# Splitting the k columns 512 and 130 instead of 322 and 320, in a TensorE-bound attention and state-space kernel

## The chip, the cores and the metric

One Trainium2 chip, one core of it. The metric is the device time of one execution in microseconds (us); a profiled execution gives the trace from which the rows in this text come. TensorE is PE in the rows, its weight loads PEld, VectorE is DVE, ScalarE is ACT, GpSimd is POOL and the queue that issues the DMAs is SP.

## What is computed

The input x has 2048 rows of 640 columns. Two branches are mixed by a gate:

```
g = sigmoid((x * gate_w).sum(-1))
a = y + x * Dskip                     # y: x convolved with K, K from A, B, C, dt
q, k, v = split(x @ wqkv)             # 32 heads of 20
pq, pk = phi(q), phi(k)               # phi(t) = (t + 1 if t > 0 else exp(t)) + 1e-6
kv = einsum(pk, v); z = pk.sum(over rows)
o = (pq @ kv) / (pq @ z + 1e-6)
out = g * a + (1 - g) * (o @ wo)
```

The kernel uses that pk.T @ v equals (pk.T @ x) @ wv: it collects G = pk.T @ x, or its transpose, over all rows, and multiplies by wv and wo afterwards.

## The kernel before

Every large product is made of three matmuls: an operand is split into a rounded high part (fp32r, a copy on ACT or DVE, `hi`) and a low part (what is left, a subtraction on DVE or POOL, `lo`), and the product is high by high, low by high and high by low (`mm3`, L105).

The kernel runs in three stages, in an order written out by hand.

**First tiles (L444 to L514).** The 2048 rows are 16 tiles of 128. The first four tiles' k is computed block by block while the blocks arrive from memory: a block is 128 of the 640 inner columns, so there are five blocks. For each block SP loads a piece of xT and of the k weights (L476 to L488), ACT, DVE and POOL split them (L489 to L496), and `k_first` (L447) issues the matmuls. Here xT is the stationary operand (128 by 128, loaded into TensorE before each matmul) and the k weights are the moving one. The 640 columns of k and the two columns of gate_w that ride along, 642 in all, are two halves: `wkA` of 322 columns (the gate's two at its end) and `wkB` of 320. Each half of each of the four tiles has a PSUM bank of its own, eight in all. `wkA` is done for all five blocks, tiles inside a block; `wkB` for blocks 0 and 1 in the same way, and for blocks 2 to 4 tile by tile at the end (L505).

**The k loop (L536 to L605).** For tile T it computes k (`k_mm`, one half, then the other, 15 matmuls each; for T of 4 and more), applies phi (`k_act`: Exp and Relu on ACT, a combination on DVE), splits pk (`k_split` on DVE), and adds tile T-1 to G: `g_main` (L220) has x as stationary operand and the first 512 columns of pk as moving one, five blocks of 3 matmuls; `g_rest` (L232) makes the other 128 columns of pk the stationary operand and has x's 640 columns as moving one, in two pieces of 320, 3 matmuls each. The order on TensorE in one turn is k half 0 of T, block 0 of `g_main`, blocks 1 and 2, k half 1 of T, `g_rest`, blocks 3 and 4. In the last turn the weights of q are split into the places that k's weights held (L561, L596): three blocks of 128 columns in `wqA`, two in `wqB`. The result of `g_rest` is then copied out (L613) and transposed on TensorE (`rem_out`, L626) into the last columns of `GT`.

**The q stage (L729 on).** A written plan interleaves q blocks, the products with wv and wo, the normalisation and the final product; its matmuls have 512 moving columns (the last output block 256 twice).

Of the kernel before, what the change touches and what calls it, by code (L numbers as in the profile page):

```python
# [30 lines left out]
F32 = mybir.dt.float32  # L31
F32R = mybir.dt.float32r
I32 = mybir.dt.int32
AF = mybir.ActivationFunctionType
# [5 lines left out]
P = 128  # L40
L = 2048
D = 640
NB = D // P
# [1 line left out]
NG = L // 512  # L45
H = 32
DH = 20
CA, CB = 320, 320
GRP = [(i * 120, min(120, D - i * 120)) for i in range(6)]
HC = 60  # L50
EPS = 1e-6
# [1 line left out]
NY = 6  # L53
NWARM = 7
N0 = 4
CONV_P = {1: (0, 1), 2: (2, 3), 3: (4,)}
CONV_K = {5: (0, 1), 6: (2, 3), 7: (4,), 8: (5, 6), 9: (7, 8), 10: (9,), 11: (10, 11), 12: (12, 13), 13: (14,)}
NK = sum(map(len, CONV_K.values()))
WQ = 3, 4, 0, 1, 2
QI = DH // NB  # L60
WKO = 40


PLAN = """
# [14 lines left out]
def body(tc, i, outT):  # L79
# [19 lines left out]
    def hi(dst, src):  # L99
        act.activation(dst, src, AF.Copy)  # L100

    def lo(dst, src, h, eng=None):
        (eng or dve).tensor_tensor(dst, src, f32(h), op=OP.subtract)  # L103
# [6 lines left out]
    def col(tag, n=NB, dt=F32):  # L110
        return pc.tile([P, n], dt, tag=tag, name=tag)

    def w_tiles(n, tag, name):
        return tuple(pc.tile([P, NB, n], F32R, tag=tag + x, name=name + x) for x in "hl")
# [22 lines left out]
    s_all = col("s_all", NT)  # L137
    ident = col("ident", P)
    bdm = col("bdm", HC)
    kvz = [col(f"kvT{k}", P) for k in range(3)]  # L140
    for v in kvz:
        pool.memset(v, 0.0)
    dtc, k0, dsk, lam, ok = [col(n) for n in ("dtc", "k0", "dsk", "lam", "ok")]
# [40 lines left out]
    kp, ke, ks = {}, {}, {}  # L184

    def k_mm(t, hf, tag="k"):
        whl, nw = (wkA, CA + 2) if hf == 0 else (wkB, CB)
        gi, o = divmod(t, 4)
        s = slice(o * P, o * P + P)
        kp[t, hf] = bank(tag)  # L190
        for b in range(NB):
            mm3(kp[t, hf][:, :nw], xTh[gi][:, b, s], xTl[gi][:, b, s],
                whl[0][:, b, :nw], whl[1][:, b, :nw], b == 0, b == NB - 1)

    def k_act(t, hf):

        p, c0, n = kp.pop((t, hf)), hf * CA, (CA, CB)[hf]
        if hf == 0:
            ke[t] = pk.tile([P, D], F32, tag="e", bufs=3, name="e")
        e = ke[t][:, c0 : c0 + n]  # L200
        r = pk.tile([P, CA], F32, tag="r", bufs=2, name="r")
        act.activation(e, p[:, :n], AF.Exp)  # L202
        act.activation(r[:, :n], p[:, :n], AF.Relu)  # L203
        if hf == 0:
            act.activation(s_all[:, t : t + 1], p[:, CA : CA + 1], AF.Copy)
        dve.scalar_tensor_tensor(e, e, 1.0, r[:, :n], op0=OP.min, op1=OP.add)  # L206

    def k_split(t):
# [23 lines left out]
    def g_rest(t):  # L232

        (xh, xl), (h, l) = xs[t], ks[t]
        if t == 0:
            for n in (0, 1):
                gps["r", n] = bank(f"r{n}")
        for n in (0, 1):
            s = slice(n * 320, n * 320 + 320)
            o = gps["r", n][:, :320]  # L240
            pe.matmul(o, h[:, 512:], xh[:, s], start=t == 0, stop=False)
            pe.matmul(o, h[:, 512:], xl[:, s], start=False, stop=False)  # L242
            pe.matmul(o, l[:, 512:], xh[:, s], start=False, stop=t == NT - 1)  # L243
# [200 lines left out]
    FIRST = {(0, 0): "g0", (0, 1): "g1", (1, 0): "g2", (1, 1): "r0",  # L444
             (2, 0): "r1", (2, 1): "g3", (3, 0): "g4", (3, 1): "k"}

    def k_first(b, hf, tiles, passes):  # L447

        w, n = ((wkA, CA + 2), (wkB, CB))[hf]
        for ps in passes:  # L450
            for t in tiles:
                if (t, hf) not in kp:
                    kp[t, hf] = bank(FIRST[t, hf])
                sl = slice(t * P, t * P + P)
                pe.matmul(kp[t, hf][:, :n], (xTl if ps == 1 else xTh)[0][:, b, sl], w[ps // 2][:, b, :n],  # L455
                          start=b + ps == 0, stop=b == NB - 1 and ps == 2)

    wkA = tuple(v[:, :, WKO : WKO + CA + 2] for v in w_tiles(3 * P, "wA", "wkA"))
    wkB = w_tiles(CB, "wB", "wkB")
    raw = {}  # L460

    x0 = {}
    xTh[0] = px.tile([P, NB, 512], F32R, tag="xh0", name="xTh0")
    xTl[0] = px.tile([P, NB, 512], F32R, tag="xl0", name="xTl0")
    cuts = {b: (0, 2, N0) if b == 0 else (0, N0) for b in range(NB)}
    pieces = {b: [slice(t0 * P, t1 * P) for t0, t1 in zip(cuts[b], cuts[b][1:])] for b in cuts}

    def wkB_load(b):
        sp.dma_start(raw[b][:, CA + 2 :], i["wkB"][b])

    def wkB_split(b):
        w = raw.pop(b)[:, CA + 2 :]
        hi(wkB[0][:, b, :], w)
        lo(wkB[1][:, b, :], w, wkB[0][:, b, :])

    for b in range(NB):  # L476
        x0[b] = pw.tile([P, 512], F32, tag="y", bufs=NY, name="x0")
        raw[b] = w_raw(b)
        for n, s in enumerate(pieces[b]):
            sp.dma_start(x0[b][:, s], i["xT"][b * P : b * P + P, s])  # L480
            if n == 0:
                sp.dma_start(raw[b][:, : CA + 2], i["wkA"][b])
        if b < 2:
            wkB_load(b)
    for b in range(2, NB):
# [1 line left out]
    x_load(0)  # L487
    x_load(1)  # L488
    for b in range(NB):  # L489
        w = raw[b][:, : CA + 2]  # L490
        for s in pieces[b]:
            hi(xTh[0][:, b, s], x0[b][:, s])
        dve.tensor_copy(wkA[0][:, b, : CA + 2], w)
        for s in pieces[b]:
            lo(xTl[0][:, b, s], x0[b][:, s], xTh[0][:, b, s])
        lo(wkA[1][:, b, : CA + 2], w, wkA[0][:, b, : CA + 2], pool)  # L496
        for t0, t1 in zip(cuts[b], cuts[b][1:]):
            k_first(b, 0, range(t0, t1), (0, 1))
        k_first(b, 0, range(N0), (2,))
        if b < 2:  # L500
            wkB_split(b)
            k_first(b, 1, range(N0), (0, 1, 2))
    for b in range(2, NB):
        wkB_split(b)
    for t in range(N0):  # L505
        for b in range(2, NB):
            k_first(b, 1, (t,), (0, 1, 2))
    for t in range(N0):
# [16 lines left out]
    def wq_lo(*a):  # L525
        src, h, l = wq_views(*a)
        lo(l, src, h)

    def wq_split(w, c, b0, b1, both=True):

        src, h, l = wq_views(w, c, b0, b1)
        hi(h, src)
        if both:
            lo(l, src, h)

    for T in range(1, NT):  # L536

        if T + 1 < NT:
            x_load(T + 1)
        if T + 3 < NT:  # L540
            xT_load(T + 3)
        for b in CONV_P.get(T, ()):
            conv_load(b)
        if T in (7, 8, 9, 10, 11):
            sp.dma_start(Wv[:, T - 7, :], i["wv"][(T - 7) * P : (T - 6) * P, :])
        if T == 14:
            for b in WQ:
                raw[b] = w_raw(b)
                sp.dma_start(raw[b][:, :CA], i["wqA"][b])
                sp.dma_start(raw[b][:, CA:D], i["wqB"][b])  # L550

        if T >= N0:
            k_mm(T, 0)
            k_act(T, 0)
        g_main(T - 1, (0,))
        if T == max(CONV_P) + 2:
            for j in range(3):
                u_load(j)
        if T >= 2:
            x_split(T)  # L560
        if T == NT - 1:  # L561
            wqA = w_tiles(3 * P, "wA", "wqA")
            for c in WQ:
                wq_split(wqA, c, 0, 3, c in WQ[:2])
        rest = (1, 2)
        if T == max(CONV_P) + 2:
            g_main(T - 1, rest[:1])
            conv_sum()
            rest = rest[1:]
        if N0 <= T + 2 < NT:  # L570
            xT_split(T + 2)
        g_main(T - 1, rest)
        if T >= N0:
            k_mm(T, 1)
            k_act(T, 1)
        if T > 1:
            k_split(T)
        g_rest(T - 1)
        g_main(T - 1, (3, 4))
        xs.pop(T - 1), ks.pop(T - 1)  # L580

        if T == 2:
            act.activation(dtc, dtc, AF.Exp)
            dve.tensor_reduce(zh, ident.rearrange("p (h i) -> p h i", i=QI), axis=AX.X, op=OP.add)
            dve.tensor_copy(bm.rearrange("p (h i) -> p h i", i=QI), zh[:, :, None].to_broadcast([P, H, QI]))
        for b in CONV_P.get(T - 1, ()):
            conv_block(b)()
        if T == max(CONV_P) + 1:
            conv_finish()
        if T == max(CONV_P) + 2:  # L590
            conv_scale()
        for j in CONV_K.get(T, ()):
            conv_out(j)
            if j + 3 < NK:
                u_load(j + 3)
        if T == NT - 1:  # L596
            wqB = w_tiles(CB, "wB", "wqB")
            for c in WQ[2:]:
                wq_lo(wqA, c, 0, 3)
            for c in WQ:  # L600
                wq_split(wqB, c, 3, NB)
                raw.pop(c)
            gates()
            for gi in range(NB):
                wo_load(gi)  # L605
# [4 lines left out]
    g_rest(NT - 1)  # L610
    g_main(NT - 1, (3, 4))
    rem = col("rem", D)
    hi(rem[:, :320], gps.pop(("r", 0))[:, :320])  # L613
    hi(rem[:, 320:], gps.pop(("r", 1))[:, :320])
    g_out(3, act)
    g_out(4, dve)
    kst.close()
# [1 line left out]

    pq = mk(top, "pq")  # L620
    pqp = mk(top, "pqp", PSUM)

    def mbank(name):
        return pqp.tile([P, 512], F32, tag="m", bufs=2, name=name)
# [11 lines left out]
    def q_block(gi, b):  # L636

        qp = pqp.tile([P, 512], F32, tag="q", bufs=3, name="qp")
        w, o = (wqA, b * P) if b < 3 else (wqB, (b - 3) * P)
        for c in range(NB):  # L640
            mm3(qp, w[0][:, c, o : o + P], w[1][:, c, o : o + P], xTh[gi][:, c, :], xTl[gi][:, c, :],
                c == 0, c == NB - 1)
# [301 lines left out]
```

## Time and profile before

| what | value |
|---|---|
| median of 3 runs | 300.05 us (299.36 to 300.11) |
| the profiled execution | 299.84 us, of which the span in the trace is 298.1 us |
| first matmul on data | 4.38 us |
| end of the first tiles' k on TensorE | 23.44 us |
| end of the last `g_main` | 146.15 us |
| busy | PE 98%, PEld 86%, DVE 77%, ACT 40%, POOL 16% |

A matmul's duration in a row is longer than what it costs in a stream, since matmuls overlap: what counts is the step from the start of one to the start of the next. The rows of the timeline merge neighbours of one kind ("x10"), so a step is a difference of starts divided by the number of matmuls between.

### The profile page before, as it was taken

How to read it: one execution, taken by the hardware profiler on the slowest of the kernel's cores; microseconds unless marked ns; L12 is line 12 of the kernel's file. 1: busy time of each engine (PE TensorE's matmuls, PEld its weight loads, DVE VectorE, ACT ScalarE, POOL GpSimd, SP SyncE). 2: the span in 40 equal slices, each digit the busy share in tenths (PEclk: the TensorE clock that was granted, in tenths of full speed). 3: DMA queues.
4: the chain of work that ended last, by engine and by line, in shares of the span. 5: the costliest groups of instructions: out<-in, count | busy, mean ns of one | idle time of the engine just before them, and what ended most of it. 6: DMA issues, size and time to landing. Idle time of an engine off the chain costs nothing.

```text
span 298.1 us, 4538 instructions
## 1 busy us (share of the span) xinstructions
PE 293.0 (98%) x1627; PEld 255.2 (86%) x1627; DVE 228.9 (77%) x355; ACT 119.0 (40%) x250; POOL 46.7 (16%) x52
## 2 busy tenths in 40 slices
PE   8999999999999999999999999999999999999994
PEld 7998899999999999999887777888888888888884
DVE  1959977799899899964843769978684778687992
ACT  3556143544545353327524464552323233313200
POOL 3605431000000000000000000003323203242531
PEclk9999999999999999999999999999999999999999
DMA  6917376065757857362264553692425122425323
GB/s 176 322 42 233 94 231 217 1 221 154 242 200 237 243 185 204 119 201 98 58 196 142 166 190 102 217 349 87 126 51 182 31 70 70 141 73 176 124 91 111
DMA packets 28409, 46.00 MB, mean 154 GB/s; under 512 B 3771, under 2 KB 10827, under 8 KB 28383
## 3 DMA queue, kind: packets, MB, share of 16 engines
q1 hardware_dynamic: 28383, 45.66, 48.6%
q8 instruction: 15, 0.25, 0.3%
q14 instruction: 11, 0.09, 0.1%
HBM read 32.92 MB, written 12.72 MB: 153 GB/s over the span
## 4 chain that ended last, share of the span: by engine, by line
PE 92%; DVE 3%; DMA 2%; issue 1%; ACT 1%; SPq 0%; DVEq 0%
PE qp L106 8%; PE fp L108 8%; PE fp L107 8%; PE fp L106 8%; PE qp L108 8%; PE qp L107 8%; PE k L107 6%; PE k L106 6%; PE k L108 6%; PE g L230 5%; PE g L228 5%; PE g L227 5%; PE g L455 3%; DMA wraw<-in_wkB 2%; PE r L242 1%; PE r L243 1%
## 5 line engine op out<-in xcount | busy, mean ns | idle before, releaser
L440 POOL TENSOR_TENSOR yb<-yb,gb 128x512 f32<-128x512 f32 x20 | 28.4, 1423 | 217.5 <-DVE acc L657 157.7
L108 PE MATMUL fp<-pTl,Mh 128*128 128x512 f32 (+1 forms) x105 | 39.8, 379 | 0.0
L107 PE MATMUL fp<-pTh,Ml 128*128 128x512 f32 (+1 forms) x105 | 39.8, 379 | 0.0
L106 PE MATMUL fp<-pTh,Mh 128*128 128x512 f32 (+1 forms) x105 | 39.8, 379 | 0.0
L651 DVE SCALAR_TENSOR_TENSOR qe<-qe,qr 128x512 f32<-128x512 f32 x20 | 15.4, 770 | 21.5 <-ACT qr L648 21.5
L228 PE MATMUL g<-ph,xl 128*128 128x512 f32 x80 | 31.5, 394 | 0.0
L227 PE MATMUL g<-ph,xh 128*128 128x512 f32 x80 | 31.4, 392 | 0.0
L202 ACT ACTIVATE e<-k 128x320 f32<-128x320 f32 x25 | 10.9, 437 | 47.1 <-PE k L108 47.1
L100 ACT ACTIVATE pTh<-qe 128x512 fp32r<-128x512 f32 x20 | 12.6, 633 | 41.7 <-DVE qe L687 41.7
L230 PE MATMUL g<-pl,xh 128*128 128x512 f32 x80 | 26.1, 391 | 0.1
L206 DVE SCALAR_TENSOR_TENSOR e<-e,r 128x320 f32<-128x320 f32 x32 | 15.9, 502 | 12.2 <-ACT r L203 12.0
L106 PE MATMUL qp<-xTh,wqAh 128*128 128x512 f32 x60 | 23.8, 396 | 0.0
L107 PE MATMUL qp<-xTh,wqAl 128*128 128x512 f32 x60 | 23.4, 390 | 0.0
L108 PE MATMUL qp<-xTl,wqAh 128*128 128x512 f32 x60 | 23.4, 389 | 0.0
L107 PEld LDWEIGHTS fp<-pTh,Ml 128*128 128x128 f32 x105 | 19.8, 188 | 3.8
L106 PEld LDWEIGHTS fp<-pTh,Mh 128*128 128x128 f32 x105 | 19.7, 188 | 3.8
L647 ACT ACTIVATE qe<-qp 128x512 f32<-128x512 f32 x20 | 11.9, 595 | 27.7 <-PE qp L108 22.7
L108 PEld LDWEIGHTS fp<-pTl,Mh 128*128 128x128 f32 x105 | 19.7, 188 | 3.7
L103 DVE TENSOR_TENSOR pTl<-qe,pTh 128x512 fp32r<-128x512 f32 x20 | 16.1, 819 | 6.8 <-ACT pTh L100 6.3
L420 DVE TENSOR_TENSOR_SCAN y<-y,cY,zero 128x512 f32<-128x512 f32 x16 | 20.5, 1278 | 0.8 <-ACT y L419 0.8
L107 PE MATMUL k<-wkAh,xTl 128*128 128x322 f32 x60 | 18.6, 310 | 0.0
L106 PE MATMUL k<-wkAh,xTh 128*128 128x322 f32 x60 | 18.6, 309 | 0.0
(168 smaller groups left out, 714.6 us busy)
## 6 DMA issues: line engine op xcount, KB each, us to landing
xraw<-in_x SPq DMA_DIRECT2D x16, 320.0 KB, 5.2
u<-in_xT SPq DMA_DIRECT2D x20, 256.0 KB, 5.4
out_T<-o SPq DMA_DIRECT2D x19, 256.0 KB, 2.5
y_d<-y SPq DMA_DIRECT2D x16, 256.0 KB, 2.3
yb<-y_d SPq DMA_DIRECT2D x16, 256.0 KB, 3.2
xTraw<-in_xTt SPq DMA_DIRECT2D x12, 320.0 KB, 4.4
Wv<-in_wv SPq DMA_DIRECT2D x5, 320.0 KB, 6.9
Mh<-M_dh SPq DMA_DIRECT2D x5, 320.0 KB, 4.7
```

What stands on the lines that cost most here:

```text
L100: act.activation(dst, src, AF.Copy)
L103: (eng or dve).tensor_tensor(dst, src, f32(h), op=OP.subtract)
L106: pe.matmul(out, ah, bh, start=start, stop=False)
L107: pe.matmul(out, al, bh, start=False, stop=False)
L108: pe.matmul(out, ah, bl, start=False, stop=stop)
L206: dve.scalar_tensor_tensor(e, e, 1.0, r[:, :n], op0=OP.min, op1=OP.add)
L227: pe.matmul(gps[b], xh[:, s], h[:, :512], start=t == 0, stop=False)
L228: pe.matmul(gps[b], xl[:, s], h[:, :512], start=False, stop=False)
L230: pe.matmul(gps[b], xh[:, b * P : b * P + P], l[:, :512], start=False, stop=t == NT - 1)
L420: dve.tensor_tensor_scan(y, y, zero.to_broadcast([P, 512]), cY[:, c], op0=OP.add, op1=OP.add)
L440: pool.tensor_tensor(ys[j], ys[j], gbs[j // NB], op=OP.mult)
L651: dve.scalar_tensor_tensor(e, e, 1.0, r, op0=OP.min, op1=OP.add)
```

## The change

The two halves of k become `wkA` of 512 columns and `wkB` of 130: the gate's two columns lead the second half, followed by k's last 128. `g_rest` has pieces of 512 and 128 columns instead of twice 320. The q weights lie as four blocks of 128 in `wqA` and one in `wqB`, and a few of their splits move from before `k_mm`'s second half to after it. In the first tiles, block 0 of the first half is loaded, split and multiplied in two column pieces of 256, tiles 0 and 1 of the first piece ahead; blocks 3 and 4 of the first half are no longer done for all four tiles, but tile by tile, just ahead of that tile's second half. One of three small zeroed tiles is made in the q stage.

```diff
-CA, CB = 320, 320
+CA, CB = 512, 128
+NB1 = 3
-WKO = 40
+QA = CA // P
+CK = CA, CB + 2
+WB = 192
...
     def k_mm(t, hf, tag="k"):
-        whl, nw = (wkA, CA + 2) if hf == 0 else (wkB, CB)
+        whl, nw = (wkA, wkB)[hf], CK[hf]
...
-        p, c0, n = kp.pop((t, hf)), hf * CA, (CA, CB)[hf]
+        kb = kp.pop((t, hf))
+        c0, n = hf * CA, (CA, CB)[hf]
+        p = kb[:, CK[hf] - n :]
...
-        if hf == 0:
-            act.activation(s_all[:, t : t + 1], p[:, CA : CA + 1], AF.Copy)
+        if hf == 1:
+            act.activation(s_all[:, t : t + 1], kb[:, :1], AF.Copy)
...
-        for n in (0, 1):
-            s = slice(n * 320, n * 320 + 320)
-            o = gps["r", n][:, :320]
+        for n, s in enumerate((slice(0, 512), slice(512, D))):
+            o = gps["r", n][:, : s.stop - s.start]
             pe.matmul(o, h[:, 512:], xh[:, s], start=t == 0, stop=False)
             pe.matmul(o, h[:, 512:], xl[:, s], start=False, stop=False)
             pe.matmul(o, l[:, 512:], xh[:, s], start=False, stop=t == NT - 1)
...
-    cuts = {b: (0, 2, N0) if b == 0 else (0, N0) for b in range(NB)}
-    pieces = {b: [slice(t0 * P, t1 * P) for t0, t1 in zip(cuts[b], cuts[b][1:])] for b in cuts}
+    cuts = {b: (0, 256, 512) if b == 0 else (0, 512) for b in range(NB)}
+    pieces = {b: [slice(c0, c1) for c0, c1 in zip(cuts[b], cuts[b][1:])] for b in cuts}
...
-        for n, s in enumerate(pieces[b]):
+        for s in pieces[b]:
             sp.dma_start(x0[b][:, s], i["xT"][b * P : b * P + P, s])
-            if n == 0:
-                sp.dma_start(raw[b][:, : CA + 2], i["wkA"][b])
+            to = slice(s.start, s.stop + 2 * (s.stop == CA))
+            sp.dma_start(raw[b][:, to], i["wkA"][b][:, to])
...
-        for t0, t1 in zip(cuts[b], cuts[b][1:]):
-            k_first(b, 0, range(t0, t1), (0, 1))
-        k_first(b, 0, range(N0), (2,))
+        for c in pieces[b] if b < NB1 else ():
+            for s in pieces[b] if c.start == 0 else (slice(0, 512),):
+                k_first(b, 0, range(s.start // P, s.stop // P), (0, 1), c)
+            k_first(b, 0, range(N0), (2,), c)
         if b < 2:
             wkB_split(b)
             k_first(b, 1, range(N0), (0, 1, 2))
...
     for t in range(N0):
+        for b in range(NB1, NB):
+            k_first(b, 0, (t,), (0, 1, 2))
         for b in range(2, NB):
             k_first(b, 1, (t,), (0, 1, 2))
...
-            wqA = w_tiles(3 * P, "wA", "wqA")
-            for c in WQ:
-                wq_split(wqA, c, 0, 3, c in WQ[:2])
+            wqA = w_tiles(CA, "wA", "wqA")
+            for c in WQ[:3]:
+                wq_split(wqA, c, 0, QA, c in WQ[:1])
...
-            for c in WQ[2:]:
-                wq_lo(wqA, c, 0, 3)
+            for c in WQ[1:]:
+                (wq_lo if c in WQ[:3] else wq_split)(wqA, c, 0, QA)
             for c in WQ:
-                wq_split(wqB, c, 3, NB)
+                wq_split(wqB, c, QA, NB)
```

The order on TensorE at the end of the first tiles, before: `wkA` of block 4 ends for the last tiles (banks r_175 and g_177), then tile 0's second half (bank g_187).

```order
L455 MATMUL r_175<-wkAl,xTh_131 128x322
L455 MATMUL g_177<-wkAl,xTh_131 128x322
L455 MATMUL g_187<-wkBh,xTh_131 128x320
L455 MATMUL g_187<-wkBh,xTl_132 128x320
L455 MATMUL g_187<-wkBl,xTh_131 128x320
L455 MATMUL g_187<-wkBh,xTh_131 128x320
```

The same place now: block 2 ends for the last tile (bank g_178), then tile 0 (banks g_170 and g_200) has its blocks 3 and 4 of the first half and its second half.

```order
L459 MATMUL g_178<-wkAl,xTh_129 128x512
L459 MATMUL g_170<-wkAh,xTh_129 128x512
L459 MATMUL g_170<-wkAh,xTl_130 128x512
L459 MATMUL g_170<-wkAl,xTh_129 128x512
L459 MATMUL g_170<-wkAh,xTh_129 128x512
L459 MATMUL g_170<-wkAh,xTl_130 128x512
L459 MATMUL g_170<-wkAl,xTh_129 128x512
L459 MATMUL g_200<-wkBh,xTh_129 128x130
L459 MATMUL g_200<-wkBh,xTl_130 128x130
L459 MATMUL g_200<-wkBl,xTh_129 128x130
```

Tile 0's first half is complete six wide matmuls into its own turn, and its second half nine narrow ones later; the other tiles' first halves wait for their own turns.

In the k loop the order of work on TensorE is the same and the widths change. Before, at the end of k's second half and in `g_rest` (banks r_418 and r_419):

```order
L108 MATMUL k<-wkBl,xTh_461 128x320
L241 MATMUL r_418<-xh,ph 128x320
L242 MATMUL r_418<-xl,ph 128x320
L243 MATMUL r_418<-xh,pl 128x320
L241 MATMUL r_419<-xh,ph 128x320
L242 MATMUL r_419<-xl,ph 128x320
L243 MATMUL r_419<-xh,pl 128x320
L227 MATMUL g_426<-ph,xh 128x512
```

The same place now, in the same turn:

```order
L111 MATMUL k<-wkBl,xTh_474 128x130
L245 MATMUL r_431<-xh,ph 128x512
L246 MATMUL r_431<-xl,ph 128x512
L247 MATMUL r_431<-xh,pl 128x512
L245 MATMUL r_432<-xh,ph 128x128
L246 MATMUL r_432<-xl,ph 128x128
L247 MATMUL r_432<-xh,pl 128x128
L232 MATMUL g_439<-ph,xh 128x512
```

No matmul came or went: of every two, one grew to 512 columns and one shrank to 130 or 128.

SP's first loads, before:

```order
L480 DMA x_133<-in_xT 128x256
L482 DMA wraw<-in_wkA 128x322
L480 DMA x_133<-in_xT 128x256
L469 DMA wraw<-in_wkB 128x320
L480 DMA x_139<-in_xT 128x512
```

SP's first loads now:

```order
L486 DMA x_131<-in_xT 128x256
L488 DMA wraw<-in_wkA 128x256
L486 DMA x_131<-in_xT 128x256
L488 DMA wraw<-in_wkA 128x258
L474 DMA wraw<-in_wkB 128x128
L486 DMA x_138<-in_xT 128x512
```

One load more stands ahead of block 1; the bytes ahead of it are the same.

More of the change, by code (lines that the diff above doesn't have):

```diff
@@ L139, in body @@
     bdm = col("bdm", HC)
-    kvz = [col(f"kvT{k}", P) for k in range(3)]
+    kvz = [col(f"kvT{k}", P) for k in range(2)]
     for v in kvz:
@@ L445, in body, with k_first @@
              (2, 0): "r1", (2, 1): "g3", (3, 0): "g4", (3, 1): "k"}
-    def k_first(b, hf, tiles, passes):
-        w, n = ((wkA, CA + 2), (wkB, CB))[hf]
+    def k_first(b, hf, tiles, passes, cols=None):
+        w, cs = (wkA, wkB)[hf], cols or slice(0, CK[hf])
         for ps in passes:
@@ L454, in k_first @@
                 sl = slice(t * P, t * P + P)
[L455 to L459, printed above, removed]
+                pe.matmul(kp[t, hf][:, cs], (xTl if ps == 1 else xTh)[0][:, b, sl], w[ps // 2][:, b, cs],
+                          start=b + ps + cs.start == 0, stop=b == NB - 1 and ps == 2)
+    wkA = w_tiles(CA, "wA", "wkA")
+    wkB = w_tiles(WB, "wB", "wkB")
     raw = {}
@@ L471, in wkB_split @@
     def wkB_split(b):
-        w = raw.pop(b)[:, CA + 2 :]
-        hi(wkB[0][:, b, :], w)
-        lo(wkB[1][:, b, :], w, wkB[0][:, b, :])
+        w = raw.pop(b)[:, CA:]
+        h, l = [v[:, b, : CK[1]] for v in wkB]
+        hi(h, w)
+        lo(l, w, h)
     for b in range(NB):
@@ L489, in body @@
     for b in range(NB):
-        w = raw[b][:, : CA + 2]
         for s in pieces[b]:
             hi(xTh[0][:, b, s], x0[b][:, s])
-        dve.tensor_copy(wkA[0][:, b, : CA + 2], w)
-        for s in pieces[b]:
+            if s.start == 0:
+                dve.tensor_copy(wkA[0][:, b, s], raw[b][:, s])
             lo(xTl[0][:, b, s], x0[b][:, s], xTh[0][:, b, s])
-        lo(wkA[1][:, b, : CA + 2], w, wkA[0][:, b, : CA + 2], pool)
-        for t0, t1 in zip(cuts[b], cuts[b][1:]):
-            k_first(b, 0, range(t0, t1), (0, 1))
-        k_first(b, 0, range(N0), (2,))
+            if s.start:
+                dve.tensor_copy(wkA[0][:, b, s], raw[b][:, s])
+            lo(wkA[1][:, b, s], raw[b][:, s], wkA[0][:, b, s], pool)
+        for c in pieces[b] if b < NB1 else ():
+            for s in pieces[b] if c.start == 0 else (slice(0, 512),):
+                k_first(b, 0, range(s.start // P, s.stop // P), (0, 1), c)
+            k_first(b, 0, range(N0), (2,), c)
         if b < 2:
@@ L596, in body @@
         if T == NT - 1:
-            wqB = w_tiles(CB, "wB", "wqB")
-            for c in WQ[2:]:
-                wq_lo(wqA, c, 0, 3)
+            wqB = w_tiles(WB, "wB", "wqB")
+            for c in WQ[1:]:
+                (wq_lo if c in WQ[:3] else wq_split)(wqA, c, 0, QA)
             for c in WQ:
-                wq_split(wqB, c, 3, NB)
+                wq_split(wqB, c, QA, NB)
                 raw.pop(c)
@@ L612, in body @@
     rem = col("rem", D)
-    hi(rem[:, :320], gps.pop(("r", 0))[:, :320])
-    hi(rem[:, 320:], gps.pop(("r", 1))[:, :320])
+    hi(rem[:, :512], gps.pop(("r", 0)))
+    hi(rem[:, 512:], gps.pop(("r", 1))[:, :P])
     g_out(3, act)
@@ L621, in body @@
     pqp = mk(top, "pqp", PSUM)
+    kvz.append(pq.tile([P, P], F32, name="kvT2"))
+    pool.memset(kvz[2], 0.0)
     def mbank(name):
@@ L638, in q_block @@
         qp = pqp.tile([P, 512], F32, tag="q", bufs=3, name="qp")
-        w, o = (wqA, b * P) if b < 3 else (wqB, (b - 3) * P)
+        w, o = (wqA, b * P) if b < QA else (wqB, (b - QA) * P)
         for c in range(NB):
```

## The prediction

> **What bounds the kernel now.** The page comes first: its busy shares and the chain that ended last.
>
> ```profile
> PE 293.0 (98%) x1627; PEld 255.2 (86%) x1627; DVE 228.9 (77%) x355; ACT 119.0 (40%) x250; POOL 46.7 (16%) x52
> PE 92%; DVE 3%; DMA 2%; issue 1%; ACT 1%; SPq 0%; DVEq 0%
> ```
>
> TensorE is busy almost throughout and carries 92% of the chain. A busy matmul can still be a stretched one, so the next view is the windows, one for T = 1 to 3 and one for the rest of the k loop.
>
> ```profile
> 23.44:36.77 13.33, 13.24 (x65) 10.99 (x64) 13.05 (x26) 5.48 (x14) 7.14 (x9) 1.00 0.51 149
> 36.77:146.15 109.38, 109.38 (x637) 101.11 (x636) 92.41 (x158) 49.86 (x115) 3.59 (x6) 1.00 0.56 174
> ```
>
> The columns are length, then PE, PEld, DVE, ACT and POOL busy. In 109 us TensorE has no idle time that the rows show. So the change is worth what it does to TensorE's steps, plus a little in the first 37 us, where VectorE too is nearly full (13.05 of 13.33).
>
> How many matmuls change is in the groups by shape: the k loop has six groups of 60 (the first and last shown), `g_rest` three of 32 (one shown), and the first tiles six kinds of 20 (for one kind, its 15 and 5).
>
> ```profile
> L107 PE MATMUL k<-wkAh,xTl 128*128 128x322 f32 x60 | 18.6, 310 | 0.0
> L106 PE MATMUL k<-wkBh,xTh 128*128 128x320 f32 x60 | 18.5, 308 | 0.0
> L243 PE MATMUL r<-xh,pl 128*128 128x320 f32 x32 | 9.9, 309 | 0.0
> L455 PE MATMUL g<-wkAl,xTh 128*128 128x322 f32 x15 | 3.8, 309 | 0.0
> L455 PE MATMUL r<-wkAl,xTh 128*128 128x322 f32 x5 | 1.5, 307 | 0.0
> ```
>
> That is 360 + 96 + 120 = 576 matmuls, or **288 pairs** of about 320 and 320, which become 288 pairs of 512 and 130 (or 128). The mean duration of one (310 ns) is not its price; the step is. The timeline gives it, first for 322 columns, then 512, then 256.
>
> ```profile
> 36.77 0.31 PE L106 MATMUL k<-wkAh,xTh 128*128 128x322 f32 x1
> ...
> 38.98 0.39 PE L227 MATMUL g<-ph,xh 128*128 128x512 f32 x1
> ...
> 155.14 0.39 PE L107 MATMUL qp<-xTh,wqAl 128*128 128x512 f32 x1
> ...
> 161.48 0.39 PE L108 MATMUL qp<-xTl,wqAh 128*128 128x512 f32 x1
> ...
> 290.44 0.28 PE L106 MATMUL fp<-pTh,Mh 128*128 128x256 f32 x1
> ...
> 293.92 0.28 PE L108 MATMUL fp<-pTl,Mh 128*128 128x256 f32 x1
> ```
>
> 15 steps in 2.21 us are 0.1473 each at 322 columns; 28 in 6.34 are 0.2264 at 512; 29 in 3.48 are 0.120 at 256. From 256 to 512 a column costs (0.2264 - 0.120) / 256 = 0.416 ns, and 0.0135 us come on top of each matmul at every width. Continued to 130 columns this line gives 0.054 + 0.0135 = **0.067 us**, and 0.2264 + 0.067 = 0.294 is what the pair costs now (2 x 0.1473 = 0.2946): by columns alone nothing changes.
>
> **The narrow step.** Whether it is 0.067 decides the case, since every matmul brings a weight load of 128 columns. Narrow matmuls stand in the trace at the start of the q stage.
>
> ```profile
> 145.92 1.31 PEld L333 LDWEIGHTS zp<-ones,zacc 128*128 128x128 f32 x10
> 146.15 1.17 PE L333 MATMUL zp<-ones,zacc 128*128 128x1 f32 x10
> 147.18 0.74 PE L630 MATMUL tp<-ident,rem 128*128 128x128 f32 x5
> 147.68 0.47 PE L106 MATMUL qp<-xTh,wqAh 128*128 128x512 f32 x1
> 150.97 0.19 PEld L342 LDWEIGHTS cp<-zsh,bm 128*128 128x128 f32 x1
> 151.19 0.17 PE L342 MATMUL cp<-zsh,bm 128*128 128x2 f32 x1
> 151.19 0.19 PEld L343 LDWEIGHTS cp<-zsl,bm 128*128 128x128 f32 x1
> 151.22 0.25 PE L343 MATMUL cp<-zsl,bm 128*128 128x2 f32 x1
> ```
>
> The ten matmuls of one column have no streaming to speak of, so their step is the load's. The first load ran under the matmul before. The second begins as the first small matmul starts (146.15), and the last ends at 145.92 + 1.31 = 147.23, so it began 0.19 earlier, at 147.04: eight steps in 0.89 us, **0.111 each**. The five of 128 columns take 0.50 us, 0.10 each. These are plain float32. The pair at 151.19 is fp32r, as k's matmuls are: the first, loaded from 150.97 on under a 512-wide matmul, takes 0.17, the second, whose load only starts at 151.19, takes 0.25. It waits for its load just as the small float32 ones do, and it leaves one record where a float32 matmul leaves two (ten for the five of zp). So a load starts when the matmul before it starts, and a step cannot be shorter than the load: 0.227 and 0.147 cover it, 0.067 does not. I take 0.111 for 130 and 128 columns.
>
> The Trainium skill ("TensorE: Matmul & The Clock Gate", section on the back-to-back issue gap) gives about 81 ns per matmul at 128 columns in a stream of loads and matmuls. Our row shows 111, and no row here shows 81; by the page the sum below would be 288 x (0.2264 + 0.081 - 0.2946) = 3.7 us.
>
> **The sum.** A pair becomes 0.2264 + 0.111 = 0.3374, that is 0.0428 more; 288 x 0.0428 = **12.3 us**, all on TensorE, which has no idle time to take it up. The order of widths does not matter: behind a wide matmul the first narrow one starts on time, but the matmul behind the last narrow one waits for its load in turn, so there are as many 0.111 steps as narrow matmuls.
>
> The first tiles. Block 0's twelve wide matmuls are 24 of 256: 12 x (2 x 0.120 - 0.2264) = 0.16 us more. The loads are these rows:
>
> ```profile
> 1.00 3.36 PE L131 MATMUL k<-ones 128*128 128x128 f32 x14 [1.00 <-POOL ones L122]
> 2.15 0.43 SPq L469 DMA_DIRECT2D wraw<-in_wkB  x1
> 2.62 0.43 SPq L480 DMA_DIRECT2D x<-in_xT  x1
> 3.90 0.33 DVE L493 CAST wkAh<-wraw 128x322 fp32r<-128x322 f32 x1 [3.90 <-DMA wraw<-in_wkA]
> 5.85 0.47 PE L455 MATMUL g<-wkAh,xTh 128*128 128x322 f32 x1
> 6.12 0.47 PE L455 MATMUL r<-wkAh,xTl 128*128 128x322 f32 x1
> 6.96 0.47 ACT L100 ACTIVATE wkBh<-wraw 128x320 fp32r<-128x320 f32 x1 [1.93 <-DMA wraw<-in_wkB]
> 7.10 0.31 PE L455 MATMUL g<-wkAl,xTh 128*128 128x322 f32 x1
> 7.49 0.41 PE L455 MATMUL g<-wkBh,xTh 128*128 128x320 f32 x1
> ```
>
> Today SP's fourth load, `wkB` of block 0, lands at 6.96 and makes TensorE step from 7.10 to 7.49 instead of 0.147: 0.24 us lost. After the change the fourth load is the second piece of block 0's first half; with it 514 of the block's 642 weight columns have come, where before it was all 642. TensorE comes to it after twelve matmuls of 256 columns, at the slow early step (0.27 for 322, so 0.21): at about 6.9. If it lands a little before 6.96, nothing is lost and the 0.24 go; if at 6.96, its cast of 0.33 costs about 0.4. I set the difference to zero, with -0.24 to +0.5 for the range. The load that SP issues in addition delays block 1 by one issue, some 0.47 us (issues at 2.15 and 2.62), and TensorE needs block 1 only after 36 matmuls of block 0.
>
> The one place where VectorE holds TensorE back in the k loop is here:
>
> ```profile
> 32.29 0.39 PE L228 MATMUL g<-ph,xl 128*128 128x512 f32 x1
> 32.76 0.50 PE L230 MATMUL g<-pl,xh 128*128 128x512 f32 x1
> 33.10 0.40 PE L227 MATMUL g<-ph,xh 128*128 128x512 f32 x1
> ```
>
> The steps are 0.47 and 0.34 instead of 0.23, 0.35 us lost to the low part of pk (`pl`). Afterwards each tile's k in the first stage ends 6 x 0.2264 + 9 x 0.111 = 2.36 us behind the one before (now nine steps of 0.147, 1.32), so VectorE begins its phi work as early as now while TensorE ends the stage about 2.5 us later. I let the 0.35 us go.
>
> What is free. The 512-wide Exp and Relu and the copies that empty the single bank of k take longer, but ScalarE waits for TensorE there, and `g_main` of three blocks (nine steps of 0.2264, 2.0 us) covers two at 0.6:
>
> ```profile
> ACT e L202 <- PE k L108: 47.1, 22, 5.6
> L647 ACT ACTIVATE qe<-qp 128x512 f32<-128x512 f32 x20 | 11.9, 595 | 27.7 <-PE qp L108 22.7
> 144.48 1.76 DVE L103 TENSOR_TENSOR wqBl<-wraw,wqBh 128x256 fp32r<-128x256 f32 x5
> ```
>
> Without that cover it would be up to 1.2 us in each of 12 turns. The q weights' splits end at 146.24 on VectorE, 1.4 us ahead of the first q matmul (147.68); more of them come after k's second half, at most about 1 us, while TensorE's way from there grows by six pairs of `g_rest`, 0.26 us. If the cover fails, that is under 0.5 us, once. The q stage's matmuls keep their widths.
>
> Sum: 12.3 + 0.16 - 0.35 = 12.1. Against the profiled execution, 299.84 us (span 298.1 and 1.7 around it, 0.2 under the median of 300.05), that is 299.84 + 12.1 = **311.9 us**.
>
> **Rivals.** *Narrow matmuls keep to their columns* (0.067): the load would hide, perhaps begun two matmuls ahead. Then the pair stays at 0.294 and only the start is left, 0.16 - 0.35 - 0.24 = -0.4: **299.4 us**, not slower. It decides as soon as a load costs no more than 0.067. For it: 0.0135 us over the columns is all that any width from 256 up shows. Against: the second fp32r matmul at 151.22, and the zp steps. Chance 0.05.
>
> *The load is hidden in part*, while the 130 columns stream: a step between 0.067 and 0.111, midway 0.089. 288 x (0.2264 + 0.089 - 0.2946) = 6.0 us, with the start's -0.2 **305.6 us**. Against it stands 0.10 for the 128-wide transposes, whose columns did not hide a load. Chance 0.07. The Trainium skill's 81 ns would lie here, at 303.4 us.
>
> *A narrow fp32r matmul runs at float32's pace.* The warm-up matmuls of 128 columns in float32 take 3.36 us for 14 records, two each, so 0.48 at the early pace, which is 0.27 / 0.147 = 1.84 times the later one: 0.26. 288 x (0.2264 + 0.26 - 0.2946) = 55 us, **355 us**. For it: no row shows an fp32r matmul between 2 and 256 columns. Against: the single record at 151.22. Chance 0.07.
>
> **How the numbers follow.** The forecast has 0.81. Its own bounds: with the mean of all ten zp steps, (147.18 - 146.15) / 10 = 0.103, it is 288 x 0.008 = 2.3 less; with 0.120, the shortest full fp32r step in the rows, 288 x 0.009 = 2.6 more; at the start 0.24 less or 0.5 more, and 0.35 more if VectorE's stall stays, 0.5 if the splits are late. That is 309.4 to 315.9. The other cases are left out, with 0.19. A difference under 0.3% (0.9 us) could not be told from none; the first rival lies there or just under it: faster 0.02, same 0.03, and slower has the rest, 0.95.
>
> **What would show it.** Right: steps of about 0.111 among the narrow `k<-wkB` matmuls, PEld rows starting as close, and turns of the k loop longer by 18 x 0.0428 = 0.77 us each; the first tiles' k ending near 26; the q stage as long as before. Wrong: narrow steps of 0.07 or above 0.13, idle time ahead of `k<-wkAh` or of `qp`, or a matmul waiting for the second piece of `wkA`.

## The result, and the profile after it

The changed kernel takes **312.0 us** in the median (311.39 to 312.19, 6 runs), beside 299.92 (299.36 to 300.28, 6 runs) for the kernel before: 12.1 us or 4.0% more, ratio 1.0401 with an interval of 1.0386 to 1.0416. The forecast was 311.9. The profiled execution of the changed kernel took 311.85 us, with a span of 310.0.

The page of the changed kernel has the same picture, longer:

```profile
PE 304.9 (98%) x1639; PEld 257.1 (83%) x1639; DVE 228.6 (74%) x356; ACT 116.6 (38%) x250; POOL 46.9 (15%) x53
PE 98%; DVE 0%; issue 0%; POOL 0%; POOLq 0%
```

TensorE gained 11.9 us of busy time, and the weight loads only 1.9, for twelve more matmuls in all: a busy sum does not tell what is waited for. By stage, before (length, then PE, PEld, DVE, ACT, POOL busy):

```profile
4.38:23.44 19.06, 18.98 (x121) 18.71 (x121) 13.14 (x23) 9.82 (x23) 5.96 (x5) 1.00 0.62 201
36.77:146.14 109.37, 109.37 (x636) 101.11 (x635) 92.40 (x158) 49.85 (x115) 3.59 (x6) 1.00 0.56 174
```

and after, the first tiles, T = 1 to 3, the rest of the k loop, and the q stage:

```profile
4.12:25.48 21.36, 21.36 (x134) 19.12 (x133) 15.43 (x29) 11.00 (x29) 8.39 (x7) 1.00 0.66 204
25.48:38.84 13.36, 13.36 (x65) 11.20 (x65) 10.57 (x21) 3.57 (x9) 6.40 (x9) 1.00 0.38 112
38.84:157.84 119.00, 119.00 (x636) 102.34 (x635) 92.78 (x158) 48.19 (x115) 3.15 (x7) 1.00 0.53 161
157.84:309.90 152.06, 148.05 (x796) 121.30 (x794) 109.41 (x150) 52.18 (x97) 27.48 (x20) 1.00 0.41 135
```

| stage | before | after | difference |
|---|---|---|---|
| start to first matmul on data | 4.38 | 4.12 | -0.26 |
| first tiles' k | 19.06 | 21.36 | +2.30 |
| T = 1 to 3 | 13.33 | 13.36 | +0.03 |
| T = 4 to the last `g_main` | 109.37 | 119.00 | +9.63 |
| from there to the end of the span | 151.9 | 152.2 | +0.2 |

The k loop pays, with exactly as many matmuls as before (x636). Its timeline shows what with: the end of k's second half in one turn, `g_rest`, and the first row of `g_main`.

```profile
45.23 0.28 PE L109 MATMUL k<-wkBh,xTh 128*128 128x130 f32 x1
...
45.80 0.27 PE L111 MATMUL k<-wkBl,xTh 128*128 128x130 f32 x1
45.91 0.44 PE L245 MATMUL r<-xh,ph 128*128 128x512 f32 x1
46.19 0.39 PE L246 MATMUL r<-xl,ph 128*128 128x512 f32 x1
46.41 0.39 PE L247 MATMUL r<-xh,pl 128*128 128x512 f32 x1
46.64 0.22 PE L245 MATMUL r<-xh,ph 128*128 128x128 f32 x1
46.70 0.27 PE L246 MATMUL r<-xl,ph 128*128 128x128 f32 x1
46.81 0.28 PE L247 MATMUL r<-xh,pl 128*128 128x128 f32 x1
46.92 0.45 PE L232 MATMUL g<-ph,xh 128*128 128x512 f32 x1
47.21 0.40 PE L233 MATMUL g<-ph,xl 128*128 128x512 f32 x1
```

and the weight loads of the same stretch:

```profile
45.51 0.19 PEld L109 LDWEIGHTS k<-wkBh,xTh 128*128 128x128 f32 x1
45.62 0.19 PEld L110 LDWEIGHTS k<-wkBh,xTl 128*128 128x128 f32 x1
45.73 0.19 PEld L111 LDWEIGHTS k<-wkBl,xTh 128*128 128x128 f32 x1
```

From 45.23 to 45.91 six narrow matmuls take 0.113 each, and their loads start 0.11 apart. The first narrow matmul behind a wide one (46.64) is followed after 0.06, since its load was ready, and the wide matmul after the last narrow one is late in its turn: from 46.92 to the next it is 0.28 or 0.29, not 0.23. No idle time is reported anywhere in this: the waiting is inside the busy rows, in durations (0.28 for 130 columns, 0.22 where the load was ready).

### The profile page after: what moved, and what is told of

Read it like the earlier page. It is cut to its first block, busy times and chain, and to the rows that moved or that the text cites. A ratio compares the mean times of both kernels' runs of the same rounds, so it can differ in the third digit from the quotient of the medians.

```text
span 310.0 us, 4569 instructions
## 1 busy us (share of the span) xinstructions
PE 304.9 (98%) x1639; PEld 257.1 (83%) x1639; DVE 228.6 (74%) x356; ACT 116.6 (38%) x250; POOL 46.9 (15%) x53
## 4 chain that ended last, share of the span: by engine, by line
PE 98%; DVE 0%; issue 0%; POOL 0%; POOLq 0%
PE qp L109 8%; PE fp L111 7%; PE fp L110 7%; PE fp L109 7%; PE qp L110 7%; PE qp L111 7%; PE k L111 7%; PE k L110 7%; PE k L109 6%; PE g L232 6%; PE g L233 6%; PE g L235 6%; PE g L459 5%; PE r L459 2%; PE r L247 2%; PE r L246 2%
## 5 line engine op out<-in xcount | busy, mean ns | idle before, releaser
L444 POOL TENSOR_TENSOR yb<-yb,gb 128x512 f32<-128x512 f32 x20 | 27.5, 1381 | 135.6 <-DMA u<-in_xT 75.0
L207 ACT ACTIVATE e<-k 128x128 f32<-128x128 f32 (+1 forms) x25 | 10.8, 432 | 69.0 <-PE k L111 69.0
L211 DVE SCALAR_TENSOR_TENSOR e<-e,r 128x512 f32<-128x512 f32 (+1 forms) x32 | 16.2, 515 | 22.7 <-ACT r L208 22.7
L232 PE MATMUL g<-ph,xh 128*128 128x512 f32 x80 | 32.2, 402 | 0.0
L109 PE MATMUL qp<-xTh,wqAh 128*128 128x512 f32 x80 | 31.7, 396 | 0.0
L110 PE MATMUL qp<-xTh,wqAl 128*128 128x512 f32 x80 | 31.2, 390 | 0.0
L111 PE MATMUL qp<-xTl,wqAh 128*128 128x512 f32 x80 | 31.1, 389 | 0.0
L109 PE MATMUL k<-wkAh,xTh 128*128 128x512 f32 x60 | 23.3, 389 | 0.0
L110 PE MATMUL k<-wkAh,xTl 128*128 128x512 f32 x60 | 23.3, 389 | 0.0
L111 PE MATMUL k<-wkAl,xTh 128*128 128x512 f32 x60 | 23.3, 389 | 0.0
L659 ACT ACTIVATE qe<-qp 128x512 f32<-128x512 f32 x20 | 11.9, 595 | 28.4 <-PE qp L111 23.5
```

The source lines that it names most:

```text
L109: pe.matmul(out, ah, bh, start=start, stop=False)
L110: pe.matmul(out, al, bh, start=False, stop=False)
L111: pe.matmul(out, ah, bl, start=False, stop=stop)
L232: pe.matmul(gps[b], xh[:, s], h[:, :512], start=t == 0, stop=False)
L444: pool.tensor_tensor(ys[j], ys[j], gbs[j // NB], op=OP.mult)
```

## The experiments

Two theories to begin with. **Load theory**, that of the prediction: a matmul's step is the longer of its streaming (0.0135 us + 0.416 ns a column) and the next weight load (0.111 us for 128 stationary columns). **Rival A**: fp32r matmuls stream slower below 256 columns; at 130 columns, twice the column time would give 0.122, which the result alone cannot tell from 0.111. Rival B, with it: loads can run further ahead than one matmul.

**k402_240 and k448_194**: the kernel before, with k split at other widths (`wkA` then begins its tile, and rows and buffers follow the widths).

```diff
-CA, CB = 320, 320
+CA, CB = 400, 240        # k448_194: 446, 194
...
```

> The kernel before with k's 642 columns in 402 and 240 (g_rest stays 320 and 320): 240 pairs. Load theory (a step is the longer of 0.0135 us + 0.416 ns a column and the weight load's 0.111 us): 0.181 + 0.113 = 0.294 against 0.2946, no change, about 299.9 us. Rival A, fp32r columns cost twice as much below 256 columns: 0.181 + 0.213, 240 x 0.10 = 24 us more, 324 us.

> The kernel before with k's 642 columns in 448 and 194. Load theory: 194 columns would stream in 0.094 but wait for the load, 0.111; pair 0.200 + 0.111 = 0.311, 240 x 0.0163 = 3.9 us more, 303.8 us. Columns alone: no change, 299.9 us. Rival A (twice the column time below 256): 0.200 + 0.175, 240 x 0.080 = 19 us more, 319 us.

Measured against 299.78 us for the kernel before: 301.79 (ratio 1.0066, 1.0049 to 1.0083) and 304.96 (1.0175, 1.0159 to 1.0192). Rival A's 324 and 319 us are out. The steps of 240 and of 194 columns, from the timelines of the two:

```profile
42.24 0.27 PE L106 MATMUL k<-wkBh,xTh 128*128 128x240 f32 x1
...
43.81 0.28 PE L108 MATMUL k<-wkBl,xTh 128*128 128x240 f32 x1
```

```profile
43.38 0.28 PE L107 MATMUL k<-wkBh,xTl 128*128 128x194 f32 x1
...
44.83 0.27 PE L108 MATMUL k<-wkBl,xTh 128*128 128x194 f32 x1
```

14 steps in 1.57 us are 0.112 at 240 columns, 13 in 1.45 are 0.112 at 194: the same as at 130. From 130 to 240 columns, width cost nothing and saved nothing here. Yet both kernels are slower than expected, by 1.9 and 1.2 us. The 1.2 us of k448_194 lie in two places of its trace: T = 1 to 3 took 14.10 us instead of 13.33, and its 448 columns stepped at 0.2027 us where 0.200 was set, 0.5 us over the k loop. The 1.9 us are taken up below.

**half_load**: the changed kernel, with half as many stationary columns in most narrow k matmuls, the moving side as it was. It leaves out part of the products for 64 rows of each tile.

```diff
...
+                m = P if first or last else 64
+                pe.matmul(kp[t, hf][:m, :nw], x[gi][:, b, o * P : o * P + m], whl[w][:, b, :nw],
...
```

> The changed kernel, where 13 of the 15 narrow k matmuls of a turn (T of 4 and more) load only 64 of the 128 stationary columns; the other 64 rows of the last 128 k columns are left without these 13 products. The moving side keeps its 130 columns. Load theory: a load of half the columns is half as long, 0.055, and the step falls to what 130 columns stream in, 0.067: 12 x 13 x 0.044 = 6.8 us less than the changed kernel, about 305.2 us. Rival A (the moving columns are slow): nothing changes, 312.0 us.

Measured: 304.1 us (303.93 to 304.47), 7.9 less than the changed kernel. From its timeline:

```profile
44.59 0.22 PE L202 MATMUL k<-wkBh,xTl 128*64 128x130 f32 x1
...
45.39 0.28 PE L202 MATMUL k<-wkBl,xTh 128*128 128x130 f32 x1
```

13 steps in 0.80 us are 0.0615 each, with the same 130 columns streamed. So the stationary side sets the narrow step. 156 x (0.1115 - 0.0615) = 7.8 us is the whole gain. Fewer stationary columns also mean fewer rows of output; that the load and not the output sets the step is in the changed kernel itself. Behind a wide matmul, a narrow one with all 128 stationary columns has its load ready, its row lasts 0.22, and the next row starts 0.06 us later (46.64 to 46.70 above, and 0.058 to 0.061 in all 17 places where 130 columns follow 512). So 128 rows of output need no 0.111.

**alternate**: the changed kernel with `g_rest` in the order 512, 128, 512, 128, 512, 128.

```diff
-        for n, s in enumerate((slice(0, 512), slice(512, D))):
...
+        for k, (w, x) in enumerate(((h, xh), (h, xl), (l, xh))):
+            for n, s in enumerate((slice(0, 512), slice(512, D))):
...
```

> The changed kernel, where g_rest alternates 512 and 128 columns instead of three and three. Load theory with one load ahead: the matmul behind each narrow one waits for its load wherever it stands, so no change, 312.0 us. Rival B, loads can run more than one matmul ahead: under a wide matmul of 0.227 two loads of 0.111 would fit, the 48 narrow steps fall from 0.111 to 0.067, 2.1 us less, 309.9 us.

Measured: 312.12 us (312.04 to 312.29). Rival B's 309.9 is out. In the timeline, neighbours of a kind merged:

```profile
46.22 0.50 PE L246 MATMUL r<-xh,ph 128*128 128x512 f32 x2
46.55 0.51 PE L246 MATMUL r<-xl,ph 128*128 128x512 f32 x2
46.90 0.51 PE L246 MATMUL r<-xh,pl 128*128 128x512 f32 x2
47.25 0.45 PE L232 MATMUL g<-ph,xh 128*128 128x512 f32 x1
```

Three pairs in 1.03 us, beside 1.01 (45.91 to 46.92) in the changed kernel's order. One load runs ahead, not two.

**rest512_only**: the kernel before with `g_rest` alone in 512 and 128.

> The kernel before with g_rest alone in 512 and 128 columns: 48 pairs. Load theory: 48 x 0.0428 = 2.1 us more, 302.0 us. Columns alone: no change, 299.9 us.

Measured: 301.72 us beside 299.81 (ratio 1.0070, 1.0058 to 1.0083), 1.9 us; its k loop took 124.61 us from the first `g_main` to the end of the last, beside 122.70. So 1.9 us of the whole come from `g_rest`, and the rest from k and its start.

**start_only**: the kernel before with the first tiles' blocks 3 and 4 tile by tile.

```diff
-        for t0, t1 in zip(cuts[b], cuts[b][1:]):
+        for t0, t1 in zip(cuts[b], cuts[b][1:]) if b < NB1 else ():
             k_first(b, 0, range(t0, t1), (0, 1))
...
     for t in range(N0):
+        for b in range(NB1, NB):
+            k_first(b, 0, (t,), (0, 1, 2))
         for b in range(2, NB):
             k_first(b, 1, (t,), (0, 1, 2))
```

> The kernel before with the first tiles' blocks 3 and 4 of the first half tile by tile, all widths as before. The prediction's step: VectorE's stall of 0.35 us near 32.3 us goes, nothing else changes: 299.6 us. Rival C: the stall has another cause than the late start of the phi work and stays, 299.9 us.

Measured: 299.38 us beside 299.81 (ratio 0.9988, 0.9977 to 0.9999). The stall is gone, and this is the same place as in the prediction (tile 2 of `g_main`):

```profile
32.14 0.39 PE L229 MATMUL g<-ph,xl 128*128 128x512 f32 x1
32.37 0.39 PE L231 MATMUL g<-pl,xh 128*128 128x512 f32 x1
32.60 0.39 PE L228 MATMUL g<-ph,xh 128*128 128x512 f32 x1
```

Steps of 0.23 where there were 0.47 and 0.34; the window T = 1 to 3 takes 12.93 us instead of 13.33. It is the one part of the change that gains, 0.4 us, and too little to be told from no change with certainty.

**start_386**: 386 and 256 columns, both wide enough to cover the load, with the same start. It was meant as a version that beats both kernels.

> The kernel before with k in 386 and 256 columns, all of it wide enough to cover the load, and blocks 3 and 4 of the first half tile by tile. Pair 0.174 + 0.120 = 0.294, no change; VectorE's stall of 0.35 us goes, and the wait of 0.24 us for block 0's second weight piece too, since TensorE comes to it later (twelve matmuls of 386 at the slow early step); the first matmul starts up to 0.2 us later, since its weights are 386 columns. Sum -0.4, 299.5 us. If the stalls stay: 300.1 us.

Measured: 301.41 us beside 299.81 (1.0056, 1.0039 to 1.0072), 1.9 us above what was expected. The k steps were 0.175 and 0.120, where 0.174 and 0.120 were set, and the k loop from T = 4 on took 0.4 us more than before; VectorE's stall was gone. The other 1.5 us were lost in the q stage, whose code was not touched: from its first product with wv to the last final matmul it took 143.9 us instead of 142.4, with the q matmuls at 0.232 instead of 0.227. The kernel with 402 and 240 columns had lost 0.8 us there too. In both, the rows of the first weight tiles had become 386 or 402 columns long (1544 and 1608 bytes); in every other kernel of this study they are multiples of 64 bytes. Hence **theory D**, that these rows slow the matmuls, and two more kernels: those with 402 and with 386 columns again, with this edit:

```diff
-WA, WB = max(3 * P, CA + 2), max(2 * P, CB)
+WA, WB = 448, max(2 * P, CB)
```

> The kernel with 402 and 240 columns again, the rows of its first weight tiles 448 columns long (1792 bytes) instead of 402 (1608 bytes), as nothing else in the kernels has rows that are no multiple of 64 bytes. Load theory as before: pairs 0.183 + 0.112 = 0.295, no change from the pairs. Theory D, uneven rows slow the matmuls that read the tile: the q matmuls on that tile fall from 0.231 to 0.227 and the q stage is 0.8 us shorter than with rows of 402; about 300.6 us are left, since VectorE's stall near 32 us is 0.7 longer than before. Otherwise 301.8 us, as with rows of 402.

> The kernel with 386 and 256 columns and the tile-by-tile start again, rows of 448 columns instead of 386. Theory D: the q stage is 1.4 us shorter than with rows of 386 and the k steps fall from 0.176 to 0.174, so that 299.5 us come out, as first expected. If the rows are not the cause: 301.4 us.

Measured, beside 299.62 us for the kernel before: 301.19 (1.0052, 1.0035 to 1.0068) and 299.90 (1.0013, 0.9996 to 1.0031). One block of q in the kernel with rows of 402:

```profile
195.27 0.40 PE L106 MATMUL qp<-xTh,wqAh 128*128 128x512 f32 x1
...
198.52 0.39 PE L108 MATMUL qp<-xTl,wqAh 128*128 128x512 f32 x1
```

and the same block with rows of 448:

```profile
195.03 0.39 PE L106 MATMUL qp<-xTh,wqAh 128*128 128x512 f32 x1
...
198.20 0.39 PE L108 MATMUL qp<-xTl,wqAh 128*128 128x512 f32 x1
```

14 steps take 3.25 us, or 0.232 each, and then 3.17, or 0.226. The q stage came back to 142.4 us in both. So the row length of the first weight tiles is the cause of the slower q stage, as theory D has it. By the whole time alone this would show in the second kernel only: 301.19 us lies midway between the 300.6 and the 301.8 that were set. Which property of the address does it stays open: 1544 and 1608 are multiples of 8 bytes and not of 16, the row lengths of the other kernels' weight tiles are all multiples of 64, and longer rows also move whatever lies behind them in memory. The k steps, in which the tile is the moving operand, did not change with the rows (0.184 at 402 columns; 0.175 and 0.176 at 386); the q steps, in which it is the stationary one, did. So the 0.174 that start_386_rows448 was to reach did not come, and it is level with the kernel before rather than ahead of it.

What was left with 402 and 240 columns, 1.6 us, stands in its own timeline and list of waits:

```profile
31.61 0.62 PE L230 MATMUL g<-pl,xh 128*128 128x512 f32 x2
32.69 0.47 PE L227 MATMUL g<-ph,xh 128*128 128x512 f32 x1 [0.46 <-DVE ph L212]
32.99 0.40 PE L228 MATMUL g<-ph,xl 128*128 128x512 f32 x1
33.52 0.50 PE L230 MATMUL g<-pl,xh 128*128 128x512 f32 x1
```

```profile
PE g L227 <- DVE ph L212: 0.5, 1, 0.5
```

Without the tile-by-tile start, VectorE's stall grew from 0.35 to 1.1 us. That the second halves at 0.112 close the four tiles faster than those at 0.147 fits this, but was not tested by itself. It is 0.75 us; the pairs are 0.184 + 0.112 = 0.296 instead of 0.294, which makes the k loop from T = 4 on 0.5 us longer (109.90 instead of 109.38); the first matmul came 0.14 later. The sum, 1.4, leaves 0.2 unassigned.

## Why the prediction was right, point by point

**The narrow step.** Taken as 0.111 from zp's loads in the trace of before; it is 0.111 to 0.113. That it is the load and not the stream was argued from zp's float32 matmuls and one fp32r matmul of two columns; half_load shows it, and k448_194 and k402_240 show where it ends, near 240 columns. The Trainium skill ("TensorE: Matmul & The Clock Gate", section on LDWEIGHTS) gives columns divided by 1.2 as nanoseconds for a load, 107 for 128 columns and 53 for 64. The step of 0.111 us is 4 ns above it; the step of 0.0615, 8 ns above it, only bounds the shorter load, since 130 columns stream in about the same time. The 81 ns at 128 columns that the Trainium skill gives on the same page (section on the back-to-back issue gap), and with it the case of 303.4 us (303.3 by its own terms), did not occur among the narrow matmuls of any kernel here.

**The sum over pairs.** 12.3 us were forecast. From T = 4 on, 219 pairs (180 of k, 39 of `g_rest`) took 9.63 us, 0.0440 each, where 0.0428 was set; alone, `g_rest`'s 48 pairs took 1.9 against 2.1. The loop's surplus over the sum is 0.26 us.

**The first tiles.** 2.73 us were set for 60 pairs and the twelve extra matmuls, with nothing for the loads; in the two profiles the stage became 2.30 longer and began 0.26 earlier. The earlier start was not in the sum. It stands in all three kernels with the changed first tiles (4.12 to 4.14, beside 4.34 and 4.38), which fits their first piece of weights, 256 columns instead of 322. The second piece was in time, cast from 5.42 on and needed at 6.38:

```profile
5.42 0.29 DVE L502 CAST wkAh<-wraw 128x256 fp32r<-128x256 f32 x1
5.55 0.39 PE L459 MATMUL r<-wkAh,xTl 128*128 128x256 f32 x1
5.78 0.28 PE L459 MATMUL g<-wkAh,xTl 128*128 128x256 f32 x1
5.90 0.40 PE L459 MATMUL g<-wkAl,xTh 128*128 128x256 f32 x2
6.38 0.40 PE L459 MATMUL g<-wkAh,xTh 128*128 128x256 f32 x2
```

But the 0.24 us that the prediction reads as lost today are no fixed cost. In rest512_only, whose first tiles are those of the kernel before, the same step is 0.15 instead of 0.39:

```profile
6.47 0.31 PE L454 MATMUL g<-wkAl,xTh 128*128 128x322 f32 x1
6.62 0.33 PE L454 MATMUL g<-wkBh,xTh 128*128 128x320 f32 x1
```

In start_only it is 0.84. The early slow steps also end at different times, near 5.9 in rest512_only and in the changed kernel, and at about 6.6 in the profile of before. So this stage took 18.15 us in rest512_only and 19.06 in the kernel before, with the same code, and 21.37, 21.62 and 21.56 in the changed kernel, half_load and alternate, which share theirs. The difference of the means is 2.9 us: whether the term of 2.73 was too large or too small can't be told from these profiles.

**VectorE's stall.** T = 1 to 3 was set at nine pairs less 0.35 us, +0.04; it is +0.03, and start_only shows the 0.4 by itself. Without this part the change would have cost about 13 us, an estimate: k448_194, narrow too and without it, took 14.10 us for T = 1 to 3, where nine pairs of `g_rest` are not even in it.

**What was to be free.** The list of TensorE's waits in the changed kernel has a single row, and it is the start:

```profile
PE k L134 <- POOL ones L125: 1.0, 1, 1.0
```

This alone would prove little, since the kernel before has the same single row and its stall of 0.35 us is not in it. The lengths say more: the loop is 0.26 us above its pairs and the rest of the span 0.2 above that of before. So the 512-wide copies out of k's single bank and the later q splits cost about 0.5 us at most, together, and the 1.2 us a turn did not come. With the additional load TensorE still went from block 0 to block 1 without a gap (8.99 to 9.11, a narrow step).

**The rivals.** The case that nothing changes needed a load of 0.067; the case in part needed loads under the stream or further ahead, which alternate and the rows exclude; float32's pace (355 us) is excluded by all the narrow steps. The first rival was also priced too high: where no load is waited for, 130 columns took 0.06 us and not the 0.067 of the line, so with hidden loads the change would have saved about 2 us more than its 299.4 says (288 x 0.007, an estimate).

**What was luck.** The mechanism was right, and so was its price. That the difference came out at 12.1 us, as forecast, is in part luck: the loop and the rest of the span took 0.5 us more than set, the start came 0.26 earlier, and the first tiles alone vary by 0.9 us between two profiles of the same code.

## What to carry to other kernels

When a product is cut into pieces along the moving side, each piece pays at least the load of its stationary operand, as these kernels show: with 128 stationary columns in fp32r that was 0.111 us, as much as about 240 moving columns, so 642 columns cost 0.294 in two nearly equal pieces and 0.338 as 512 and 130. Look for it in the distance between starts, since a TensorE that waits for loads is reported as busy, and price a new width by a matmul of that kind in the old trace, however small.

## What the runs showed of the hardware that was not expected

- The line through 256, 322 and 512 columns (0.0135 us and 0.416 ns a column) does not hold for narrower matmuls that wait for no load. 130 columns took 0.058 to 0.061 us behind a wide matmul and 0.0615 in half_load, where the line gives 0.067; 194 columns took 0.087 behind a wide matmul in k448_194, where it gives 0.094. Between, at 402 and 448 columns, the steps of 0.184 and 0.203 were 0.003 above it. Why was not tried.
- Two kernels whose weight tiles had rows of 1544 and 1608 bytes ran untouched q matmuls at about 0.232 us instead of 0.227, which cost 1.5 and 0.8 us in the q stage; with rows of 1792 bytes that was gone. With rows of 1544 bytes even the matmuls on the second, evenly rowed tile were slow (14 steps from 205.26 to 208.51):

```profile
205.26 0.40 PE L107 MATMUL qp<-xTh,wqBh 128*128 128x512 f32 x1
...
208.51 0.40 PE L109 MATMUL qp<-xTl,wqBh 128*128 128x512 f32 x1
```

Why the second tile suffers in that kernel, and not in the one with 1608 bytes, was not settled.
